# Banded attention with a routed expert layer: the key copy moves from VectorE to ScalarE, and two pieces of work change places

## The chip, the cores and the metric

The kernel runs on one core of a Trainium2 chip. The metric is device time in microseconds (us). Five engines work side by side, each through its own queue in program order: PE (TensorE, matrix products and transposes into the accumulator memory PSUM), DVE (VectorE), ACT (ScalarE), POOL (GpSimd, which also issues the gathers and scatters here) and SP (SyncE, which issues the loads). They wait for each other through semaphores. Buffers come from pools: a pool with three buffers lets the fourth tile start only when the first is no longer read.

## The reference

Two layers follow each other. The first is attention with a causal band of 96 keys, plus the first 8 keys for everyone, and a bias that falls with distance; the second sends each token to one of eight experts.

```python
# q, k, v: (4, 8, 768, 64): batch, heads, tokens, width
scores = (q @ k.T) / sqrt(64) + bias         # kept only where the key is global or local
a = exp(scores - max) / (sum + 1e-9)
x = (a @ v) as (3072, 512)                   # tokens by heads*width
logits = x @ w_gate                          # (3072, 8)
e = argmax(logits); gate = softmax(logits)[e]
out = gate * (relu(x @ w1[e]) @ w2[e])       # w1: (8, 512, 1024), w2: (8, 1024, 512)
```

## The kernel before

Tokens are taken in 24 blocks of 128 (N = 24), six to a batch (NBLK = 6). A block looks at its own keys (t = 1 in the tiles) and at the block before it (t = 0; a copy `ka` in which the first 32 columns hold the first keys of the batch). The first block of a batch has only t = 1. The loop is software-pipelined: step n makes scores of block n, prepares queries and keys of block n + 1, makes values of block n - 1 and tokens (rows of x, and logits) of block n - 2.

```python
def prep_q(n):                      # transpose on PE, copy out of PSUM on ACT
    transposed(ps_t, qts[n][:], rawt[n]["q"], "act", QS)

def prep_k(n):
    # ...
    transposed(ps_t, kts[n][:], rawt[n]["k"], "dve")      # L242 is the DVE copy in it
    # ...                           # for most blocks POOL then copies kts into ka (L294, L295)

def transposed(ps, dst, src, on, scale=1.0):
    pt = ps.tile([P, NPAIR, P], F32, tag="t", name="pt")  # one of 3 PSUM buffers "t"
    for m in range(NPAIR):
        nc.tensor.transpose(pt[:, m, :], src[...], ident[:])
    if on == "act":
        nc.scalar.activation(dst, pt[:], AF.Copy, bias=0.0, scale=scale)   # L240
    else:
        nc.vector.tensor_copy(out=dst, in_=pt[:])                          # L242

def scores(n):                      # two groups g of four heads
    # ... products into PSUM tile sp (L358), then on DVE:
    nc.vector.tensor_tensor(z, sc, bi, ALU.add)           # bias, p <- sp (L372), 128x1024
    ps[n].append(p)

def exps(n):
    for p in ps[n]:
        nc.scalar.activation(z, z, AF.Exp)                # L379, one for each group

def both(n):                        # the sums' addends: t = 0 and t = 1 added, on DVE
    if n % NBLK == 0:
        return
    for p in ps[n]:
        nc.vector.tensor_tensor(t, z[:, :, 0, :], z[:, :, 1, :], ALU.add)  # pb (L388)

def values(n):
    for m in range(NPAIR):
        # ... products p x v into po, a PSUM buffer "t", two m to a buffer (L400)
        if m % 2:
            nc.scalar.copy(ots[n][:, m - 1:m + 1], po[:, 0:2])             # L404
    pr = ps_r.tile(...)             # the only PSUM buffer "r"
    # ... sums of the exponentials from pb into pr (L410), logits from ots into pr (L414)
    nc.scalar.copy(rs[:], pr[:, 0, :])                    # L417

def tokens(n, rs):
    nc.tensor.transpose(pr[:, 1, :], rs[:], ident[:])     # L425
    # ... four transposes of ots into px (L428), a PSUM buffer "t"
    # ... on DVE: den, rden, lh (L434, L436, L439: den and lh read pr), lg (L442), xr <- px (L445)
```

The step before the change, cut to what matters. `choose` and `gates` pick the expert of a finished batch, `dispatch` ranks its tokens, and `send` scatters two blocks of rows to their experts' places in memory.

```python
for n in range(N + 1):
    if n < N: scores(n)
    if n + 1 < N: prep_q(n + 1)
    if n < N and n != 1: exps(n)
    if n == 2: both(1)
    if n == 0: biases(1, (0, 1, 2, 3), "act")
    # ... n == 2: memory is cleared on POOL; n == 3: ex.numbers, nine small DVE operations
    if n + 1 < N: prep_k(n + 1)
    # ... load(n + 3), pieces of the experts' weights, send()
    if n >= 2: tokens(n - 2, rs.pop(n - 2))      # and gates() at a batch's turn
    if n < N and n != 1: both(n)
    if n == N:
        ex.x_in_s(0, ps_t.tile(...))             # the early tile: transposes (L791), copy to xsT
    if n: rs[n - 1] = values(n - 1)
    if n == 1: exps(n)
    if n < N: mix_v(n)                           # POOL puts the first rows of v into a block
    # ... n == 22: send(); ex.early(), which gathers the early tile's rows into xs
    # ... dispatch at a batch's turn
# ... tokens(N - 1), and then the experts, beginning with
ex.up_s(0, 0, ex.xsT[0], ex.u[0])                # L800: the early tile's first products
```

The "early tile" holds up to 128 rows of expert 0, and a second one those of expert 1, from the first three batches, so that PE can begin on them while the last batch is still being dispatched.

Of the kernel before, what the change touches and what calls it, by code (L numbers as in the profile page):

```python
# [23 lines left out]
def kernel(  # L24
# [208 lines left out]
    def transposed(ps, dst, src, on, scale=1.0):  # L233

        pt = ps.tile([P, NPAIR, P], F32, tag="t", name="pt")
        for m in range(NPAIR):
            nc.tensor.transpose(pt[:, m, :], src[:, 2 * m:2 * m + 2, :].rearrange("p a d -> p (a d)"),  # L237
                                ident[:])
# [4 lines that stand above are left out]
# [7 lines left out]
    def banded(stack, rt, pool, rows, ex, den_all):  # L250
# [6 lines left out]
        ps_t = stack.enter_context(tc.tile_pool(name="ps_t", bufs=3, space=bass.MemoryType.PSUM))  # L257
        ps_r = stack.enter_context(tc.tile_pool(name="ps_r", bufs=1, space=bass.MemoryType.PSUM))

        rawt, kts, kas, qts, vts, ps, ots, prs, seqs = {}, {}, {}, {}, {}, {}, {}, {}, {}  # L260
        pbs = {}
        N = B * NBLK

        def load(n):
            b, i = divmod(n, NBLK)

            kind = dict(tag="vt0") if i == 0 else dict(tag="vt", bufs=6)
            vts[n] = seq.tile([P, H, D], F32, name="vt", **kind)
            r = rawt[n] = {}
            for nm, src in (("q", q), ("k", k)):  # L270
                r[nm] = raw.tile([P, H, D], F32, tag=nm, name=f"raw_{nm}")
                nc.sync.dma_start(out=r[nm][:], in_=src[b, :, ts(i, P), :].rearrange("h p d -> p h d"))
            nc.sync.dma_start(out=vts[n][:], in_=v[b, :, ts(i, P), :].rearrange("h p d -> p h d"))

        def mix_v(n):

            i = n % NBLK
            if i > 1:
                nc.gpsimd.tensor_copy(out=vts[n - 1][0:GW], in_=vts[n - i][0:GW])

        def prep_q(n):
            qts[n] = raw.tile([P, NPAIR, P], F32, tag="qt", bufs=2, name="qt")
            transposed(ps_t, qts[n][:], rawt[n]["q"], "act", QS)

        def prep_k(n):
            b, i = divmod(n, NBLK)
            kind = dict(tag="kt0") if i == 0 else dict(tag="kt", bufs=3)
            kts[n] = seq.tile([P, NPAIR, P], F32, name="kt", **kind)
            transposed(ps_t, kts[n][:], rawt[n]["k"], "dve")
            if i == 0:  # L290
                kas[n + 1] = kts[n][:]
            elif i + 1 < NBLK:
                t = raw.tile([P, NPAIR, P], F32, tag="ka", bufs=2, name="ka")
                nc.gpsimd.tensor_copy(out=t[:, :, GW:P], in_=kts[n][:, :, GW:P])  # L294
                nc.gpsimd.tensor_copy(out=t[:, :, 0:GW], in_=kts[n - i][:, :, 0:GW])  # L295
                kas[n + 1] = t[:]
# [36 lines left out]
        def biases(which, heads, on):  # L333
            for h in heads:
                g, j, a = h // 4, h // 2 % 2, h % 2
                dst, src = ((first[:, g, a, j], dist[:, 0]) if which == 0 else
                            (other[:, g, a, j], dist[:, 1:3]))
                if on == "act":
                    nc.scalar.activation(dst, src, AF.Copy, bias=0.0, scale=-slopes[h])
                else:  # L340
                    nc.gpsimd.tensor_scalar(dst, src, -slopes[h], None, ALU.mult)
# [30 lines left out]
                    nc.vector.tensor_tensor(z, sc, bi, ALU.add)  # L372
                ps[n].append(p)

        def exps(n):
            for p in ps[n]:
                z = p[:].rearrange("p a j t c -> p (a j) t c")
                z = z[:, :, 1, :] if n % NBLK == 0 else p[:].rearrange("p a j t c -> p (a j t c)")
                nc.scalar.activation(z, z, AF.Exp)  # L379

        def both(n):
# [4 lines that stand above are left out]
                t = work.tile([P, 2, 2, P], F32, tag="pb", bufs=4, name="pb")  # L386
                z = p[:].rearrange("p a j t c -> p (a j) t c")
                nc.vector.tensor_tensor(t[:].rearrange("p a j c -> p (a j) c"), z[:, :, 0, :], z[:, :, 1, :],  # L388
                                        ALU.add)
                pbs.setdefault(n, []).append(t[:])  # L390

        def values(n):
            vals = [(t, vts[n - 1 + t]) for t in range(n % NBLK == 0, 2)]
            ots[n] = work.tile([P, NPAIR, P], F32, tag="ot", name="ot")
            for m in range(NPAIR):
                if m % 2 == 0:
                    po = ps_t.tile([P, NPAIR, P], F32, tag="t", name="po")
                for x, (t, vt) in enumerate(vals):
                    for a in range(2):
                        nc.tensor.matmul(po[D * a:D * a + D, m % 2, :], lhsT=vt[:, 2 * m + a, :],  # L400
                                         rhs=ps[n][m // 2][:, a, m % 2, t, :], start=(x == 0),
                                         stop=(x == len(vals) - 1), skip_group_check=True)
                if m % 2:
                    nc.scalar.copy(ots[n][:, m - 1:m + 1], po[:, 0:2])  # L404

            pr = prs[n] = ps_r.tile([P, 4, P], F32, tag="r", name="pr")
            all_p = pbs.pop(n, None) or [p[:, :, :, 1, :] for p in ps[n]]
            for a in range(2):
                for m in range(NPAIR):
                    nc.tensor.matmul(pr[GW * m:GW * m + GW, 0, :], lhsT=one_in[:, a, :],  # L410
                                     rhs=all_p[m // 2][:, a, m % 2, :], start=(a == 0),
                                     stop=False, skip_group_check=True)
            for m in range(NPAIR):
                nc.tensor.matmul(pr[GW * m:GW * m + GW, 0, :], lhsT=gate_w[:, m, :], rhs=ots[n][:, m, :],  # L414
                                 start=False, stop=True, skip_group_check=True)
            rs = work.tile([P, P], F32, tag="rs", name="rs")
            nc.scalar.copy(rs[:], pr[:, 0, :])  # L417
            del ps[n]
            return rs
# [45 lines left out]
        def send():  # L465
            for _ in range(min(2, len(sends))):
                sends.pop(0)()

        rs = {}
        for n in range(N + 1):  # L470
            if n < N:
                scores(n)
            if n + 1 < N:
                prep_q(n + 1)
            if n < N and n != 1:
                exps(n)
            if n == 2:
                both(1)
            if n == 0:
                biases(1, (0, 1, 2, 3), "act")  # L480
            if n == 2:
                numbers = ex.clear_s()
            if n == 3:
                ex.numbers(*numbers)
            if n in (3, 4):
                biases(0, range(4 * n - 12, 4 * n - 8), "pool")
            if n + 1 < N:
                prep_k(n + 1)
            if n == 0:
                spare = ps_r.tile([P, 512], F32, tag="r", name="spare")  # L490
                for _ in range(4):
                    nc.tensor.matmul(spare[:], lhsT=idle[:, 0:P], rhs=idle[:], start=True, stop=True)
            if n + 3 < N:
                load(n + 3)
            for load_ in feed.pop(n, ()):
                load_()

            if n - 2 < N - NBLK + 2:
                send()
            b, i = divmod(n - 2, NBLK)  # L500
            if n >= 2:
                tokens(n - 2, rs.pop(n - 2))
                if i == 0 and b:
                    xr, _, oh, gates = seqs[b - 1]
                    gates()
            if n < N and n != 1:
                both(n)
            if n == N:
                ex.x_in_s(0, ps_t.tile([P, NPAIR, P], F32, tag="t", name="pt"))
            if n:  # L510
                rs[n - 1] = values(n - 1)
            if n == 1:
                exps(n)
            if n < N:
                mix_v(n)
            if i == 2 and b == B - 1:
                send()
                ex.early()
            if i == 0 and b > 0:
                sends += dispatch(pool, ps_t.tile([P, 512], F32, tag="t", name="pr"), rt, xr, oh)  # L520
                if b == B - 1:
                    send()
# [807 lines left out]
```

## Time and profile before

The median of three runs is 521.93 us (521.83 to 522.01); the profiled execution spans 522.3 us.

| engine | busy us | share of the span | instructions |
|---|---|---|---|
| PE | 504.2 | 97% | 5019 |
| PE weight loads | 423.7 | 81% | 5019 |
| DVE | 327.5 | 63% | 688 |
| ACT | 147.5 | 28% | 298 |
| POOL | 188.4 | 36% | 285 |

The busy time of an engine is the union of its instructions' spans. PE's instructions overlap, and a busy PE need not be at its peak. The shares are an average over the attention part (to about 161 us), a passage (to 171 us) and the experts (to the end). A list of groups gives, for each line, engine and tile, the summed busy time and the mean of one instruction: on the whole span the key copy L242 and query copy L240 take 682 and 598 ns each, the bias add L372 1218 ns, an addend's add L388 761 ns, an exponential over 1024 columns 1050 ns. DVE's instructions overlap a little at their edges, so two bias adds in a row take 2.36 us.

The chain of waits is followed back from the last instruction: at each step to what released it, or to the instruction before it on its engine. "Issue" in it is time in which nothing that the profile shows was waited for.

### The profile page before, as it was taken

Reading aid. Unit: us, or ns where it says so; the run is one execution under the profiler, and the core shown is the slowest. Engines: PE = TensorE matmul, PEld = TensorE weight load, DVE = VectorE, ACT = ScalarE, POOL = GpSimd, SP = SyncE. Lnnn points to the kernel's source line nnn. Section 1 sums busy time; section 2 is a strip of 40 time slices with the busy share of each in tenths; the row PEclk is TensorE's granted clock in tenths of the full one; section 3 lists DMA queues with packets and bytes.
Section 4 is the critical chain, followed back from the end, with each engine's and each line's share of the span. In section 5 each row is a group of like instructions: output and inputs, shape, how many; then the busy total and the mean of one; then the engine's idle time right before and its main releaser. Section 6 shows DMA issues by size and latency. Waiting matters only on the chain.

```text
span 522.3 us, 12395 instructions
## 1 busy us (share of the span) xinstructions
PE 504.2 (97%) x5019; PEld 423.7 (81%) x5019; DVE 327.5 (63%) x688; ACT 147.5 (28%) x298; POOL 188.4 (36%) x285
## 2 busy tenths in 40 slices
PE   7999999999997999999999999999999999999994
PEld 4888888888885778679899879969969878996984
DVE  5898978978985656817778258326707804832741
ACT  3555545544542101212212112112201211211120
POOL 5431161161253465306366055115307304511503
PEclk9999999999998999999999999999999999999998
DMA  9999798799922222037083452028156007400101
GB/s 185 214 221 213 164 217 226 165 217 227 303 98 71 97 79 82 8 140 278 21 312 125 163 187 94 2 95 333 31 204 216 26 1 261 175 2 23 43 4 50
DMA packets 96332, 72.75 MB, mean 139 GB/s; under 512 B 79324, under 2 KB 79326, under 8 KB 96228
## 3 DMA queue, kind: packets, MB, share of 16 engines
q1 hardware_dynamic: 87808, 52.44, 36.8%
q0 software_dynamic: 7872, 19.01, 10.7%
q8 instruction: 54, 0.88, 0.7%
q14 instruction: 50, 0.41, 0.3%
q10 hardware_dynamic: 548, 0.02, 0.1%
HBM read 61.46 MB, written 14.73 MB: 146 GB/s over the span
## 4 chain that ended last, share of the span: by engine, by line
PE 79%; DVE 10%; issue 7%; DMA 1%; POOL 1%; POOLq 0%; ACT 0%; DVEq 0%; ACTq 0%
PE u L972 18%; PE u L800 10%; PE d L1034 9%; PE d L1043 7%; PE u L810 7%; PE sp L358 5%; PE po L400 5%; DVE p L372 5%; PE d L810 3%; PE u L1141 2%; PE u L1116 2%; PE pt L237 2%; PE pr L410 2%; DVE kt L242 2%; PE t L952 2%
## 5 line engine op out<-in xcount | busy, mean ns | idle before, releaser
L1050 DVE TENSOR_TENSOR UV<-UV,d 128x512 f32<-128x512 f32 x8 | 5.5, 688 | 110.9 <-ACT yu L1144 81.3
L734 POOL DMA_INDIRECT out_dram<-ys,to_u x8 | 8.3, 1039 | 142.6 <-ACT yu L1144 87.6
L372 DVE TENSOR_TENSOR p<-sp,other 128x1024 f32<-128x1024 f32 x40 | 47.0, 1218 | 16.6 <-PE sp L358 15.1
L800 PEld LDWEIGHTS u<-xsT,w 128*128 128x128 f32 x448 | 50.9, 192 | 1.8 <-DVE c L942 0.8
L400 PE MATMUL po<-p,vt 128*64 128x128 f32 x704 | 48.6, 284 | 3.7 <-DVE kt L242 3.0
L800 PE MATMUL u<-xsT,w 128*128 128x128 f32 x448 | 51.7, 276 | 0.0
L400 PEld LDWEIGHTS po<-p,vt 128*64 128x64 f32 x704 | 39.1, 140 | 11.8 <-DVE kt L242 7.0
L972 PE MATMUL u<-cx,c 128*128 128x128 f32 x384 | 48.1, 275 | 0.0
L379 ACT ACTIVATE p<-p 128x1024 f32<-128x1024 f32 (+1 forms) x48 | 45.1, 979 | 4.3 <-DVE p L372 3.0
L972 PEld LDWEIGHTS u<-cx,c 128*128 128x128 f32 x384 | 45.5, 192 | 0.0
L358 PE MATMUL sp<-qt,kt 64*128 64x128 f32 x448 | 39.0, 277 | 1.0 <-DVE kt L242 0.9
L972 PE MATMUL u<-xT,w 128*128 128x128 f32 x256 | 39.4, 276 | 0.2 <-issue 0.2
L972 PEld LDWEIGHTS u<-xT,w 128*128 128x128 f32 x256 | 34.2, 192 | 1.3 <-DVE y L1064 0.4
L810 PE MATMUL u<-w,huT 128*128 128x512 f32 x80 | 35.1, 592 | 0.0
L358 PEld LDWEIGHTS sp<-qt,kt 64*128 64x128 f32 x448 | 31.6, 188 | 3.1 <-issue 1.2
L1034 PE MATMUL d<-c,ch 128*128 128x256 f32 x128 | 32.8, 379 | 0.0
L215 POOL DMA_INDIRECT xs_dram<-xr,slot_i x24 | 25.0, 1042 | 19.3 <-DVE cnt L862 10.8
L294 POOL COPY ka<-kt 128x384 f32<-128x384 f32 x16 | 8.1, 506 | 65.2 <-DVE den_all L434 62.8
L810 PEld LDWEIGHTS u<-w,huT 128*128 128x128 f32 x80 | 15.2, 190 | 17.0 <-issue 16.7
L388 DVE TENSOR_TENSOR pb<-p 128x512 f32<-128x512 f32 x40 | 28.8, 761 | 0.0
L240 ACT ACTIVATE qt<-pt 128x512 f32<-128x512 f32 x24 | 14.4, 598 | 47.2 <-PE pt L237 44.7
L358 PE MATMUL sp<-qt,ka 64*128 64x128 f32 x256 | 27.4, 285 | 0.1
(254 smaller groups left out, 1026.2 us busy)
## 6 DMA issues: line engine op xcount, KB each, us to landing
w<-in_moe_w_dram SPq DMA_DIRECT2D x24, 1024.0 KB
w<-in_moe_w_dram SPq DMA_DIRECT2D x16, 512.0 KB
raw_q<-in_q_dram SPq DMA_DIRECT2D x24, 256.0 KB
raw_k<-in_k_dram SPq DMA_DIRECT2D x24, 256.0 KB
vt<-in_v_dram SPq DMA_DIRECT2D x24, 256.0 KB
xs_dram<-xr,slot_i POOLq DMA_INDIRECT x24
xg<-xs_dram,grow POOLq DMA_INDIRECT x16
mu<-xs_dram,grow_e POOLq DMA_INDIRECT x16
```

Source lines behind the costliest of these rows:

```text
L215: d = nc.gpsimd.indirect_dma_start(out=xs_dram[:], out_offset=bass.IndirectOffsetOnAxis(ap=slot_i[:, u:u + 1], axis=0), in_=xr[:, u, :].bi ...
L240: nc.scalar.activation(dst, pt[:], AF.Copy, bias=0.0, scale=scale)
L358: nc.tensor.matmul(sp[:, a, j, t, :], lhsT=kt[r, m, :], rhs=qts[n][r, m, :], start=True, stop=True, skip_group_check=True)
L372: nc.vector.tensor_tensor(z, sc, bi, ALU.add)
L379: nc.scalar.activation(z, z, AF.Exp)
L388: nc.vector.tensor_tensor(t[:].rearrange("p a j c -> p (a j) c"), z[:, :, 0, :], z[:, :, 1, :], ALU.add)
L400: nc.tensor.matmul(po[D * a:D * a + D, m % 2, :], lhsT=vt[:, 2 * m + a, :], rhs=ps[n][m // 2][:, a, m % 2, t, :], start=(x == 0), stop=(x ...
L800: nc.tensor.matmul(ph[:, i, :], lhsT=self.w[e % 2][0][:, c, ts(half * HF + i, P)], rhs=xT[:, c, :], start=(c == 0), stop=(c == NDC - 1), s ...
L810: nc.tensor.matmul(py[:].rearrange("p a b -> p (a b)"), lhsT=h[:, f, :], rhs=self.w[e % 2][1][:, f, :], start=(f == 0), stop=(f == NFC - 1 ...
L972: nc.tensor.matmul(bank[:, r, :], lhsT=lhs(k), rhs=rhs(k), start=first, stop=True, skip_group_check=True)
L1034: nc.tensor.matmul(self.half(i, j), lhsT=lhs, rhs=rhs, start=(f == 0 and j == 0), stop=True, skip_group_check=True)
L1043: nc.tensor.matmul(self.half(i, j), lhsT=lhs(f), rhs=rhs(f), start=False, stop=True, skip_group_check=True)
```

## The change

Three things move. The copy of the transposed keys out of PSUM goes from DVE to ACT for all blocks but the first, to relieve DVE, whose copy stood behind the bias adds. The sums' addends (`both`) are made one step later, ahead of the token chain, when their exponentials are long done; the second group's exponential goes behind the copies of the values and the sums on ACT. And at the end the early tile's transposes go behind the last block's values, so that PE works on those values while the gather is under way.

```diff
-            transposed(ps_t, kts[n][:], rawt[n]["k"], "dve")
+            transposed(ps_t, kts[n][:], rawt[n]["k"], "act" if n else "dve")
 ...
-        def exps(n):
-            for p in ps[n]:
+        def exps(n, groups):
+            for p in ps[n][groups]:
 ...
-            if n < N and n != 1:
-                exps(n)
-            if n == 2:
-                both(1)
-            if n == 0:
-                biases(1, (0, 1, 2, 3), "act")
             if n == 2:
                 numbers = ex.clear_s()
             if n == 3:
                 ex.numbers(*numbers)
             if n in (3, 4):
                 biases(0, range(4 * n - 12, 4 * n - 8), "pool")
+            if 0 < n <= N:
+                both(n - 1)
             if n + 1 < N:
                 prep_k(n + 1)
+            if n < N and n != 1:
+                exps(n, slice(0, 1 if n else 2))
+            if n == 0:
+                biases(1, (0, 1, 2, 3), "act")
 ...
-            if n < N and n != 1:
-                both(n)
+            if n:
+                rs[n - 1] = values(n - 1)
+            if 0 < n < N:
+                exps(n, slice(n != 1, 2))
             if n == N:
                 ex.x_in_s(0, ps_t.tile([P, NPAIR, P], F32, tag="t", name="pt"))
-            if n:
-                rs[n - 1] = values(n - 1)
-            if n == 1:
-                exps(n)
```

In the changed kernel ACT's order in a step is: query copy, key copy, first exponential, two output copies, sums' copy, second exponential. DVE's is: two bias adds, two addends' adds of the block before, the token chain.

## The prediction

> **What bounds the kernel now.** I read the busy shares first, then stretches of the span, then the chain of waits, then the list of waits. The page's first part gives PE 97% of the span, with DVE at 63% and ACT at 28%, so the first question is where the missing 3% of PE lie. The stretches tell (columns: stretch, its length, then busy us of PE, PEld, DVE, ACT, POOL with counts of instructions, the granted PE clock, the DMA share and GB/s):
>
> ```profile
> 33.00:40.00 7.00, 7.00 (x109) 6.28 (x107) 6.59 (x11) 4.05 (x8) 1.09 (x1) 1.00 0.90 221
> ...
> 101.00:108.00 7.00, 6.50 (x103) 5.60 (x103) 6.79 (x18) 3.38 (x6) 1.73 (x3) 1.00 0.61 120
> ...
> 161.00:167.00 6.00, 3.46 (x29) 2.82 (x29) 2.90 (x10) 0.27 (x1) 3.46 (x4) 0.81 0.33 88
> 167.00:171.00 4.00, 3.58 (x52) 3.14 (x49) 0.68 (x4) 1.01 (x3) 0.00 (x0) 0.87 0.00 0
> 171.00:522.00 351.00, 343.38 (x2681) 288.99 (x2679) 187.98 (x371) 65.08 (x145) 130.21 (x170) 1.00 0.32 113
> ```
>
> The reader is to see three regimes. Attention up to 161 us has PE full, but in some stretches DVE is as full (6.79 of 7 at 101 to 108). At 161 to 171 PE stands still for some 3 us and then runs at a clock of 0.81 to 0.87. From 171 on the experts keep PE at 98%; nothing of the change lies there, so whatever is gained before 171 moves the end by as much.
>
> The chain of waits shows what ends last in the first two regimes (columns: start, us, what):
>
> ```profile
> 103.09 0.92 DVE p L372
> 104.01 0.14 issue
> 104.14 1.21 DVE p L372
> 105.35 0.61 DVE kt L242
> 105.97 0.04 issue
> 106.01 1.09 PE po L400 x16
> 107.10 0.57 PE pr L410 x16
> ...
> 160.76 3.50 DMA xs<-xs_dram,grow_s
> 164.27 0.14 issue
> 164.40 0.85 PE pt L791 x4
> 165.26 3.29 PE po L400 x32
> 168.55 0.57 PE pr L410 x16
> ```
>
> In step 15 (scores of block 15) the chain leaves PE: two bias adds on DVE, then the key copy behind them in DVE's queue, and only then the second half of the values' products, whose PSUM buffer the key copy had to free. Near the end the gather of the early tile's rows lands at 164.27, its transposes follow, and the last block's values stand behind them though their inputs were ready long before. The list of waits up to 170 us (who waited for whom: us in total, times, longest) names the same two:
>
> ```profile
> PE po L400 <- DVE kt L242: 3.0, 7, 0.8
> PE pt L791 <- DMA xs<-xs_dram,grow_s: 2.1, 1, 2.1
> ```
>
> **What the skill says.** The Trainium skill, "SBUF — State Buffer", section "Who interferes with whom", has it that a DVE instruction with two SBUF inputs contends with a GpSimd instruction that reads SBUF. The addends' add (L388) is such a one, and the trace agrees: a pair takes 1.28 us alone (107.34) but 1.59 us at 81.85, beside POOL's copy of the values at 81.69. "ScalarE: Activation LUTs", section "Table sets: the hidden batching unit", says that copy is in every table set, so a copy between two exponentials costs no switch; the trace agrees, as queries are copied by ACT (0.60) and exponentials follow without a gap. "TensorE: Matmul & The Clock Gate", section "Part 1: The HAM clock gate", says that an idle PE falls to half its clock; here 3 us of waiting brought the mean clock to 0.81, and 32 products of the values took 3.29 us where 1.90 is usual.
>
> **The change part by part.** PE's work in a full step, from the chain at 30 to 43 us, where PE alone is on it: scores 1.99, transposes of q and k 1.02, of sums and outputs 0.11 and 0.44, values 1.90, sums 0.57, logits 0.31: 6.34 us, and full steps there follow each other at 6.33 (30.22, 36.55). Later full steps take 6.85 to 7.05 (100.86, 107.92, 114.92, 121.96), a full set of six 39.5 (54.49 to 94.03).
>
> First, the key copy leaves DVE. DVE's step is two bias adds 2.36, key copy 0.61, the token chain (0.09, 0.21, 0.24, 0.27, 0.60, with gaps 1.55) and two addends' adds 1.20: 5.7 us, 5.1 without the copy. The two steps at each batch's turn add 1.1 (choice of expert) and 1.8 (gates and ranks). ACT's step grows from 3.6 (query copy 0.55, exponentials 1.95, three copies 1.0) to 4.2 of 6.3, so it doesn't bind.
>
> Second, the addends. They now stand between the bias adds and the token chain, 1.20 us earlier than that chain, and in place of 0.61. So the last read of the sums' bank by the token chain (lh, L439) ends some 0.6 later in a step than now: before 4.73 after the step's start, after 5.33. PE wants that single bank for the next sums at 5.45. It just fits; any DVE delay over 0.1 us lands on PE there. This is my main doubt: the wait for the key copy can come back as a wait for the bank.
>
> Third, the second exponential goes behind the copies of values and sums in ACT's queue, so these no longer stand behind two exponentials. In the first step after a batch's turn (the short values, 6.16 us where PE has 5.4) the outputs' copy starts 5.13 into the step only because of this; after: query and key copies to 3.9, one exponential to 4.9, copy. Gain 0.25 in three steps.
>
> Sum over attention. Start: block 1's scores waited 0.6 to 0.9 for the key copy behind the first bias adds: 0.6 gained. Step 2 took 7.33 with the copy late: gains 0.65, as 0.35 of the 1.0 returns through POOL's copies of the same key, which start at about 4.0 now and meet the addends. Step 3 has nine small DVE operations (0.85) ahead of the addends now: loses 0.4. Together 0.85. In each later set of six: 0 in the half step, 0.25 in the next, 0 and 0.1 in the two with POOL's key copies beside the addends, 0.5 and 0 in the two with scatters, where the bias add starts only 2.1 into the step instead of 1.2. There bank arithmetic gives 2.1 + 2.36 + 1.20 + 0.65 = 6.3, past 5.45, so about today's 7.0 stays in one of them. That is 0.85 for a set, and with two sets and a part (0.4) before step 22: 0.85 + 1.7 + 0.4 = about 2.9.
>
> Fourth, the tail. Now the values of the last block (3.29), sums and logits (0.9) and the wait for their copy stand between the transposes at 164.40 and the experts' first product at 170.46. After, they come before the transposes. From the start of step 22 (147.47) I count 6.6 and 7.2 for steps 22 and 23 with the bank's wait, then 0.5 for the copy of the sums, 0.55 transposes, 1.9 values, 0.95 sums and logits: transposes at 165.2. The gather follows the values of block 21, whose products end 0.8 earlier in their step, so it lands at about 163.5 and is hidden. Then 0.44 for transposes at full clock and 0.7 for DVE's copy, under which the last token's transposes lie: experts from about 166.3, against 170.5. Gain 4.2, besides the 2.9. The experts' chain of dispatch follows the same products as before, so it moves along.
>
> Total 4.2 + 2.9 = 7.1; 521.9 - 7.1 = 514.8, taken as 514.7.
>
> **Rivals.** (a) The bank binds in all the full steps: PE waits for the sums' bank where it waited for the key copy, attention gains nothing, only the tail is left: 517.7. For it: only 0.1 us of slack, and a collision costs 0.3. Against it: without scatters or POOL copies DVE has over a microsecond free in a step. (b) DVE's relief comes through: all steps run at PE's 6.34, with 6.6 at the turn. That is about 39.5 - 37.5 = 2 a set, some 5.5 in attention, and the last steps too are nearer PE's own work, so that the tail gives 5: 511.5. For it: stretches such as 33 to 40 with PE at 7.00 of 7. Against it: the late bias adds beside scatters have another cause than the key copy. (c) Loads bind once steps shrink: 1.28 MB in a step with a piece of weights takes 6 us at the 213 to 221 GB/s of the early slices. But loads are issued three steps ahead and only one wait on keys is listed, so under 1 us. (d) PE goes on waiting for the gather because scatters do not come earlier: transposes can't precede 163.5, costing nothing unless attention gains over 2 more.
>
> **Range and chances.** Tail alone gives 517.7; a tail spoilt by 1 us, 518.7; all at PE's pace 511.5, a little better with the wait at 164 gone 510.8. I put 8 in 10 on 510.8 to 518.7. Faster by over 2% needs 511.5 or less, the whole of rival (b): 0.17. Within 2%: 0.80. Slower by over 2% would need 10 us lost, which no row suggests: 0.03.
>
> **What would show it.** Right: the key copy no longer ends waits of the values' products; the first expert product starts near 163.5 (166.3 less 2.9); the clock stays at 1.00 through the tail; the wait for the gather is near nothing. The bank: waits of the sums (L410) for lh or pb, some 0.3 to 0.8 each in steps with scatters or key copies on POOL. Wrong: steps of 6.4 beside scatters (then faster), sums waiting in every step (then 517 or more), or experts that don't follow the earlier start because a gather or a weight load takes over after 171.

## The result and the profile after

The changed kernel takes 515.35 us (median of five runs, 514.19 to 516.26) against 522.01 us (521.83 to 522.22) for the kernel before: ratio 0.9873, 95% interval 0.9856 to 0.9891. Predicted were 514.7 us, in a range of 510.8 to 518.7.

One caution comes first. The profiled executions are single ones: that of before spans 522.3 us and took 524.06 us in all, 2.05 above the median; that of after spans 514.3 us and took 516.22, 0.87 above its median. So the two traces stand 8.0 us apart and the medians 6.7. The extra 1.3 us belong to the executions, and the differences below, which come from the traces, are by so much too large in sum.

The busy shares (first part of the page, kernel after):

```profile
PE 498.3 (97%) x5019; PEld 423.2 (82%) x5019; DVE 313.2 (61%) x665; ACT 159.4 (31%) x321; POOL 189.4 (37%) x285
```

Twenty-three copies moved from DVE to ACT: DVE has 14.3 us less work and ACT 11.9 more. PE's share is 97% as before, and its instructions are as many, yet they count 5.9 us less busy time; only 2.1 of the 8.0 us are idle time that went. PE's instructions overlap, so when they follow each other more slowly they can still leave no gap, and the busy share hides the wait: step 7 took 6.16 us before and 5.70 after, with no more than 0.03 us idle in either. The counts in the stretches show it. Step 16, one with scatters, before:

```profile
108.00:115.00 7.00, 6.96 (x103) 5.94 (x103) 5.52 (x11) 3.39 (x6) 4.42 (x6) 1.00 0.76 189
```

The same step after, and what follows it (columns as in the prediction):

```profile
104.00:111.00 7.00, 7.00 (x124) 6.14 (x115) 5.28 (x10) 4.08 (x8) 4.58 (x7) 1.00 0.92 215
...
155.00:160.00 5.00, 3.62 (x33) 3.38 (x35) 2.11 (x7) 1.28 (x2) 2.99 (x3) 0.66 0.40 105
160.00:165.00 5.00, 4.82 (x61) 4.13 (x58) 2.76 (x13) 0.88 (x3) 0.00 (x0) 1.00 0.01 3
165.00:514.00 349.00, 341.65 (x2666) 287.40 (x2665) 186.47 (x365) 65.07 (x144) 129.21 (x170) 1.00 0.33 114
```

PE counts as busy for all but 0.04 of the 7 us in both, but in them it now gets through 124 instructions in place of 103. (The stretch 101 to 108 in the prediction is step 15, one with POOL's key copies.) The end of attention keeps a hole: 3.62 of 5 us at 155 to 160, at a clock of 0.66. From 165 on nothing has changed: from the experts' first product to the end are 351.8 us before and 351.6 after.

The list of waits up to 175 us (after) names what PE waits for now:

```profile
PE pr L410 <- DVE lh L439: 4.3, 9, 1.1
...
PE po L400 <- POOL vt L279: 1.4, 1, 1.4
```

The waits of the values for the key copy (3.0 us) and of the transposes for the gather (2.1 us) are gone. In their place stand nine waits of the sums for the last read of their only bank (in steps 2, 3, 8, 9, 14, 15, 20, 21 and 23), and one wait for a copy on POOL. The second is seen in the chain at the end of attention (after; start, us, what):

```profile
153.24 0.35 POOL xs L724
...
154.60 1.33 POOL xs L724
155.94 1.16 POOL vt L279
...
157.15 3.31 PE po L400 x32
160.46 0.57 PE pr L410 x16
161.03 0.31 PE pr L414 x6
161.34 0.60 PE pt L789 x4
161.97 0.70 DVE xsT L790
...
162.71 3.84 PE u L798 x32
```

The two gathers of the early tiles are issued at 153.24 and 154.60. The copy that puts the first rows of v into the last block stands behind both in POOL's queue and ends at 157.10; only then do the last values start. The trace of before already has this copy behind both gathers (POOL, before):

```profile
160.76 1.17 POOL L726 DMA_INDIRECT xs<-xs_dram,grow_s  x1 [3.72 <-DVE xr L445]
162.24 1.00 POOL L726 DMA_INDIRECT xs<-xs_dram,grow_s  x1 [0.30 <-issue]
163.25 0.62 POOL L279 COPY vt<-vt 32x512 f32<-32x512 f32 x1
```

It ended at 163.87 there, 0.4 us before the gather landed.

Laid out by steps (from one step's first scores to the next one's; computed from the start times in the two traces), the gain before step 22 is 5.6 us, 0.2 of it ahead of step 2:

| step | before us | after us | what lies in it |
|---|---|---|---|
| 2 and 3 | 7.33, 6.96 | 6.58, 7.38 | first key copies; nine small DVE operations in step 3 |
| 4, 5 | 6.34, 6.34 | 6.34, 6.34 | nothing besides |
| 7, 13, 19 | 6.16 each | 5.70 each | short values |
| 8, 14, 20 | 6.85, 6.84, 6.85 | 6.84 each | key copies on POOL, choice of expert |
| 9, 15, 21 | 7.00, 7.05, 7.06 | 6.64, 6.77, 6.83 | key copies on POOL |
| 10, 11, 16, 17 | 7.04, 7.04, 7.00, 7.03 | 6.34, 6.33, 6.34, 6.34 | scatters |

From the start of step 22 to the experts' first product are 23.0 us before (147.47 to 170.46) and 20.8 after (141.89 to 162.71): 2.2 us more.

### The profile page after: what moved, and what is told of

Its sections match the earlier page's. It is cut to its first block, busy times and chain, and to the rows that moved or that the text cites. A ratio compares the mean times of both kernels' runs of the same rounds, so it can differ in the third digit from the quotient of the medians.

```text
span 514.3 us, 12403 instructions
## 1 busy us (share of the span) xinstructions
PE 498.3 (97%) x5019; PEld 423.2 (82%) x5019; DVE 313.2 (61%) x665; ACT 159.4 (31%) x321; POOL 189.4 (37%) x285
## 4 chain that ended last, share of the span: by engine, by line
PE 82%; DVE 10%; issue 6%; POOL 1%; POOLq 0%; DVEq 0%
PE u L970 18%; PE u L798 10%; PE d L1032 9%; PE d L1041 7%; PE u L808 7%; PE sp L358 6%; PE po L400 5%; DVE p L372 4%; PE pt L237 3%; DVE pb L388 3%; PE d L808 3%; PE u L1139 3%; PE u L1114 3%; PE pr L410 2%; PE t L950 2%
## 5 line engine op out<-in xcount | busy, mean ns | idle before, releaser
L379 ACT ACTIVATE p<-p 128x1024 f32<-128x1024 f32 (+1 forms) x48 | 47.3, 988 | 1.4 <-DVE p L372 1.1
L400 PE MATMUL po<-p,vt 128*64 128x128 f32 x704 | 45.1, 281 | 1.4 <-POOL vt L279 1.4
L358 PE MATMUL sp<-qt,kt 64*128 64x128 f32 x448 | 37.9, 275 | 0.9 <-DVE kt L242 0.9
L215 POOL DMA_INDIRECT xs_dram<-xr,slot_i x24 | 23.8, 993 | 17.9 <-DVE cnt L860 9.9
L294 POOL COPY ka<-kt 128x384 f32<-128x384 f32 x16 | 9.2, 576 | 56.2 <-ACT kt L240 56.2
L997 ACT COPY uv<-u 128x256 f32<-128x256 f32 x32 | 11.9, 373 | 51.2 <-PE u L970 51.1
L1032 PEld LDWEIGHTS d<-c,ch 128*128 128x128 f32 x128 | 24.3, 190 | 3.3
```

The lines of the kernel that those rows point to most:

```text
L215: d = nc.gpsimd.indirect_dma_start(out=xs_dram[:], out_offset=bass.IndirectOffsetOnAxis(ap=slot_i[:, u:u + 1], axis=0), in_=xr[:, u, :].bi ...
L358: nc.tensor.matmul(sp[:, a, j, t, :], lhsT=kt[r, m, :], rhs=qts[n][r, m, :], start=True, stop=True, skip_group_check=True)
L1032: nc.tensor.matmul(self.half(i, j), lhsT=lhs, rhs=rhs, start=(f == 0 and j == 0), stop=True, skip_group_check=True)
```

## The experiments

Twelve runs follow, four on each of three chips; each is compared with runs of the kernel before on the same chip (medians 522.93, 523.67 and 521.80 us). Of these chips the changed kernel itself ran on the third alone. Three questions: do the parts of the change need each other, what is the reorder of the early tile worth, and why do the steps with scatters run at PE's pace?

**The key copy alone.** The kernel before with only this edit:

```diff
-            transposed(ps_t, kts[n][:], rawt[n]["k"], "dve")
+            transposed(ps_t, kts[n][:], rawt[n]["k"], "act" if n else "dve")
```

> The kernel before with one line of the change: keys copied by ACT, all else as before. Theory (the parts of the change need each other): in ACT's queue the key copy now stands behind both exponentials and ends some 5.8 us into the step, so the second half of the values' products, which takes the key's PSUM buffer, starts there instead of at 4.5, and full steps take about 7.5 us: 530 to 540 us in all. Rival (the relief of DVE carries the attention's gain by itself): steps near 6.4, 515 to 518 us.

Measured: 540.36 us, ratio 1.0322 (1.0274 to 1.0369), at the upper end of what was expected: the copy alone costs 17 us. The waits up to 165 us (key copy alone) show where:

```profile
PE po L400 <- DVE xr L445: 13.1, 15, 1.8
PE po L400 <- ACT kt L240: 3.0, 5, 1.1
```

In the chain of this kernel one exponential runs at 67.58 and the key copy at 68.53, some 5.1 us into its step, because both exponentials stand before it in ACT's queue. The transposed keys hold one of the three PSUM buffers until that copy ends. In 15 of these 20 waits the second half of the values' products starts as soon as `xr` has read the tokens' buffer, so it seems to take that one instead: in step 5 this read ends at 5.04 us, where the key copy ended at 4.16 in the kernel before. The split of the exponentials is no extra; without it the copy must not move.

**The other moves without the copy.** The changed kernel with the key copy back on DVE:

```diff
-            transposed(ps_t, kts[n][:], rawt[n]["k"], "act" if n else "dve")
+            transposed(ps_t, kts[n][:], rawt[n]["k"], "dve")
```

> The changed kernel with the key copy given back to DVE. Theory: DVE does bias adds, addends, key copy and then the token chain; the key copy ends 5.4 into the step and the last read of the sums' bank 6.0, so full steps take about 7.2 us: 524 to 530 us. Rival (it was only the addends and their meeting with the scatters that cost time): 515 to 517 us.

Measured: 530.72 us, ratio 1.0136 (1.0093 to 1.0179), a little more than expected. The chain (changed kernel with keys on DVE) shows a full step:

```profile
68.12 1.05 PE po L400 x16
...
69.25 0.38 ACT ot L404
69.63 0.04 issue
69.67 1.09 PE po L400 x16
```

Now the key copy stands behind the two addends on DVE, its buffer is still held, and PE must wait for the copy of its own first outputs before it can go on (0.5 us in the step shown; 8.6 us in 15 times up to 165 us). So the copy and the new order of the loop each lose alone, and win only together.

**The early tile's reorder alone.** The kernel before with the transposes of the early tile moved behind the last values:

```diff
-            if n == N:
-                ex.x_in_s(0, ps_t.tile([P, NPAIR, P], F32, tag="t", name="pt"))
             if n:
                 rs[n - 1] = values(n - 1)
             ...
+            if n == N:
+                ex.x_in_s(0, ps_t.tile([P, NPAIR, P], F32, tag="t", name="pt"))
```

> The kernel before with the early tile's transposes behind the last block's values, nothing else. Theory (POOL's copy of the first value rows stands in its queue behind the two gathers, so the last values cannot start before it): gain of 0.5 to 1.5 us, 520.5 to 521.5 us, with PE waiting for vt instead of for the gather. Rival (the tail is worth what was predicted, 4.2): 517 to 518 us.

Measured: 521.97 us against 522.93, ratio 0.9975 (0.9957 to 0.9993): 1 us. The chain (reorder alone) gives the reason in two lines:

```profile
163.54 0.63 POOL vt L279
...
164.21 3.57 PE po L400 x32
```

The values no longer wait for the gather's data, but for POOL to get past the gathers' issue to the copy behind them, which is hardly earlier: 164.21 where the transposes began at 164.40 before.

**The change without that reorder.** The changed kernel with the transposes ahead of the values again ran on two chips.

```diff
+            if n == N:
+                ex.x_in_s(0, ps_t.tile([P, NPAIR, P], F32, tag="t", name="pt"))
             if n:
                 rs[n - 1] = values(n - 1)
             ...
-            if n == N:
-                ex.x_in_s(0, ps_t.tile([P, NPAIR, P], F32, tag="t", name="pt"))
```

> The changed kernel with the early tile's transposes put back ahead of the last block's values. Theory (same): within 0.7 us of the changed kernel, 515 to 516.5 us. Rival (the move brings 2 to 4 us): 517.5 to 519.5 us.

On the first chip: 520.96 us, ratio 0.9962 (0.9946 to 0.9978), outside both expectations: a much smaller gain than the change's, and by more than the reorder could explain. Its trace showed why: the steps with scatters (10, 11, 16, 17, 22) took 6.84, 7.49, 7.87, 7.65 and 6.83 us. So the run does not measure the reorder, and it raised the third question. On the third chip it ran again, beside the changed kernel itself:

> The changed kernel itself, beside its variants on one chip. Theory (the stall beside the scatters depends on the run or the chip, not on the order of the variant): here the steps of blocks 10, 11, 16, 17 and 22 also take more than 6.34 us, by 0.5 to 1.5 each, and the time is 517 to 521 us, above the 515.35 of its first runs. Rival (the stall came from the edits of the variants, as none of their runs was free of it): steps of 6.34 and 515 to 516 us.

> The changed kernel with the early tile's transposes ahead of the last block's values again, beside the changed kernel on the same chip. The passage alone was worth 1 us on the kernel before (521.97 against 522.93). Theory: here it is worth 0 to 2 us: 0 to 2 us slower than the changed kernel, because values that wait for POOL's copy or for a late step give part of it back. The prediction's own figure was 4.2 slower.

The changed kernel: 515.33 us (514.05 to 517.38), ratio 0.9881 (0.9861 to 0.9901), as in its first runs and not the 517 to 521 of the theory. Without the reorder: 516.28 us (515.25 to 519.22), ratio 0.9907 (0.9884 to 0.9929). The same program took 520.96 on the first chip, so its edit is not what stalls the steps with scatters. The intervals overlap; the medians lie 0.95 us apart, and the traces 0.6 us at the start of the experts' first product (161.95 and 161.32). Without the reorder (chain, third chip) the transposes wait for the gather's data:

```profile
153.24 3.40 DMA xs<-xs_dram,grow_s
156.63 0.14 issue
156.77 0.63 PE pt L789 x4
157.40 1.05 PE po L400 x16
...
162.11 3.57 PE u L798 x32
```

With it (the changed kernel, same chip) the values wait for POOL's copy and start 0.3 us before that:

```profile
155.89 1.16 POOL vt L279
...
157.10 1.97 PE po L400 x32
...
161.32 3.84 PE u L798 x32
```

So the reorder is worth about 1 us: in the kernel before that is clear of the noise, in the changed kernel it is not. Most of the 4.2 is not in it.

**The copy between the gathers.** The changed kernel with the second gather issued behind the last values' copy on POOL:

```diff
-            for e in range(NS):
-                self.gather(self.xs[:, e, :], self.grow_s[:, e:e + 1])
+            self.gather(self.xs[:, 0, :], self.grow_s[:, 0:1])
...
+            if n == N - 1:                       # behind mix_v(n) and early()
+                ex.gather(ex.xs[:, 1, :], ex.grow_s[:, 1:2])
```

> The changed kernel with POOL's copy of the first value rows for the last block put between the two gathers of the early tiles; the second gather, needed much later, is issued after it. Theory (that copy's place in POOL's queue holds the last values up, 1.4 us of wait and then products at a low clock, 3.3 us for 1.9): last values start near 155.6, early tile's first product near 160, gain of 2 to 3.5 us over the changed kernel: 512 to 513.5 us. Rival (the last values are held by the second exponential or the sums' copy, or PE would be cold anyway): within 0.7 us of 515.3.

Measured on the second chip: 522.76 us, ratio 0.9972 (0.9957 to 0.9988): a clear miss. Its steps with scatters took 6.90, 7.62, 8.70, 7.75 and 6.86 us, so PE came to the last values only at 164.09, long after POOL's copy, and the edit had nothing to gain. It is judged in the last kernel below.

**The addends before POOL's key copies.** The changed kernel, with POOL reading a corner of the second addend before it copies keys, so that the two no longer overlap:

```diff
+                if n - 2 in pbs:
+                    nc.gpsimd.tensor_copy(out=scr[:], in_=pbs[n - 2][1][:, 0, 0, 0:8])
                 nc.gpsimd.tensor_copy(out=t[:, :, GW:P], in_=kts[n][:, :, GW:P])
```

> The changed kernel in which POOL first reads a corner of the addends (eight columns, a tiny copy) before it copies the keys for the next block, so that its copies no longer run beside the addends' adds. Theory (two readers of SBUF, DVE's two-input add and POOL, shut each other out for 0.3 us, and the token chain then frees the sums' bank late): in steps 2, 8, 14 and 20 and the steps after the turn, the pair of adds takes 1.28 instead of 1.59 us, the sums start near 5.5 instead of 5.8 to 6.0, 1.5 to 2.5 us less: 513 to 514 us. Rival (the bank's wait is not set by that meeting, or the later key copy delays the next scores): 515 to 517 us.

Measured on the second chip: 520.74 us, ratio 0.9942 (0.9925 to 0.9960), well above both expectations. In the aimed steps the theory held: steps 2, 8 and 9 went from 6.58, 6.84 and 6.64 to 6.34, 6.60 and 6.34 us, and a pair of addends from 1.59 to 1.28 us. This is what the Trainium skill, "SBUF — State Buffer", section "Who interferes with whom", leads one to expect, and 0.3 us a pair is its size here. But the steps with scatters took 7.62, 7.17, 10.25, 7.43 and 7.64 us, and ate it.

**Where the scatters lie.** Two kernels, each run once on the second chip, ask whether it matters when in a step a scatter is issued. In the kernel before, POOL was made to wait for the next queries, so that the scatters of the first two batches come in the middle of a step:

```diff
-            if n - 2 < N - NBLK + 2:
+            if n - 2 < N - NBLK + 2 and (n % NBLK != 3 or n > 18):
+                if sends and n < 18:
+                    nc.gpsimd.tensor_copy(out=scr[:], in_=qts[n + 1][:, 0, 0:8])
                 send()
```

> The kernel before in which the scatters of batches 1 and 2 are moved inside the step: not in steps 9 and 15 but in 10, 11, 12 and 16, 17, 18, and in 10, 11, 12, 16 and 17 POOL first reads a corner of the query copy, so that they run at about 3.4 to 6 us of the step, away from the addends' adds at 6.5 to 7.8. The third batch's scatters stay where they were. Theory (a scatter that meets an addends' add holds up what other engines learn of PE by 1 to 2 us): in steps 10, 11, 16 and 17 the first bias add starts 1.2 into the step and these steps take 6.3 to 6.5 instead of 7.0, while steps 22 and 23 keep 2.1: 519 to 520 us. Rival (scatters delay PE's signals wherever they lie): bias adds still late or other waits in the same steps, 521 to 523 us.

Measured: 529.05 us, above both expectations. The late bias adds of steps 10, 11, 16 and 17 went (1.21 us into the step in place of 2.1), but the steps grew to 7.18, 7.87, 7.80 and 7.86 us. Steps 22 and 23, whose scatters had not moved, kept 2.1. What is late now is ACT's second copy of the values' outputs: it starts 6.41, 7.10, 7.03 and 7.09 us into these steps, though PE's products end at 5.52, as in step 5, where the copy starts at 5.57. In the changed kernel POOL was made to wait for the next keys, which puts the scatters beside the addends:

```diff
+                if sends and n % NBLK in (4, 5):
+                    nc.gpsimd.tensor_copy(out=scr[:], in_=kts[n + 1][:, 0, 0:8])
                 send()
```

> The changed kernel in which, in steps 10, 11, 16, 17 (and 22), POOL first reads a corner of the key copy, so that the scatters start at about 4.0 into the step, beside the addends' adds at 3.5 to 4.8. Theory (meeting of scatter and addends' add): the adds take 1.5 or more, a scatter 1.2 instead of 0.98, signals of PE reach ACT or DVE 1 us late, and these four steps take 6.7 to 7.4 instead of 6.34: 516.5 to 519 us. Rival (only a port is shared for 0.3 us): the steps take at most 6.6, 515 to 516.5 us.

Measured: 518.66 us, steps 10, 11, 16, 17 and 22 at 7.51, 6.83, 6.86, 6.86 and 6.84. These are the times expected from a meeting of scatters and addends, but not its signs: in steps 10 and 16, where the two meet, a pair of adds takes 1.29 and 1.28 us, as it does alone. And the bias adds are late (1.8) in steps 10, 16 and 22, which still have a scatter 0.1 to 0.35 us after their start, and on time (1.21) in steps 11 and 17, whose scatters all come at 4.7 and later. There it is again ACT's second copy that is late. Step 11 (begins at 74.40; timeline of PE, POOL and ACT):

```profile
77.96 1.97 PE L401 MATMUL po<-p,vt 128*64 128x128 f32 x32
...
79.09 0.98 POOL L215 DMA_INDIRECT xs_dram<-xr,slot_i  x1 [0.48 <-issue]
...
80.46 0.37 ACT L405 COPY ot<-po 128x256 f32<-128x256 f32 x1 [0.94 <-PE po L401]
```

and the same step of the changed kernel (begins at 73.31; after):

```profile
76.86 1.97 PE L400 MATMUL po<-p,vt 128*64 128x128 f32 x32
...
78.87 0.37 ACT L404 COPY ot<-po 128x256 f32<-128x256 f32 x1 [0.45 <-PE po L400]
```

PE's products end 5.52 us into the step in both; the copy follows at 6.06 in the one and 5.57 in the other. So in these two kernels, each run once, the delay goes where the scatters go, and a meeting with the addends is not needed for it.

The same for the bias add is seen when one step of the same loop is compared on two chips. Step 17, without the reorder of the early tile, first chip (timeline: start, us, engine, line, operation; in brackets how long the engine stood idle, and for whom):

```profile
113.93 0.49 PE L358 MATMUL sp<-qt,ka 64*128 64x128 f32 x4
...
114.92 0.39 PE L358 MATMUL sp<-qt,ka 64*128 64x128 f32 x4
114.94 0.97 POOL L215 DMA_INDIRECT xs_dram<-xr,slot_i  x1 [0.30 <-issue]
...
116.51 2.36 DVE L372 TENSOR_TENSOR p<-sp,other 128x1024 f32<-128x1024 f32 x2 [2.62 <-PE sp L358]
```

and the changed kernel, third chip:

```profile
110.68 0.49 PE L358 MATMUL sp<-qt,ka 64*128 64x128 f32 x4
...
111.89 2.36 DVE L372 TENSOR_TENSOR p<-sp,other 128x1024 f32<-128x1024 f32 x2 [1.31 <-PE sp L358]
112.00 0.97 POOL L215 DMA_INDIRECT xs_dram<-xr,slot_i  x1 [0.30 <-issue]
```

PE makes the scores in the same time in both; the bias add follows 2.6 us after their start on the first chip and 1.2 us on the third. DVE was idle and waited for PE's signal alone. Steps 4 and 5, which have no scatters beside them, are at 6.34 us in both traces.

**The scatters two steps later.** The changed kernel with the scatters of the first two batches sent beside blocks 12, 13, 18 and 19:

```diff
-            if n - 2 < N - NBLK + 2:
+            if n - 2 < N - NBLK + 2 and n not in (9, 10, 15, 16):
                 send()
```

> The changed kernel with the scatters of the first two batches sent two steps later, so that their traffic lies beside blocks 12, 13, 18 and 19, whose steps have spare time on DVE. Theory (PE's signals come late while the scatters' traffic runs, wherever it lies): steps 10, 11, 16 and 17 go to 6.34 us even if they stall in the changed kernel on this chip, and steps 12, 13, 18 and 19 grow by 0 to 1 us each; in sum 0 to 3 us faster than the changed kernel. Rival (the late bias adds of those steps have another cause than the scatters, say the loads that lie there): steps 10, 11, 16, 17 stay as they are in the changed kernel.

Measured: 518.15 us (515.22 to 519.53), ratio 0.9915 (0.9887 to 0.9943), so 2.8 slower than the changed kernel on this chip, where 0 to 3 faster was expected. The question itself got no answer, since on this chip the changed kernel's steps 10, 11, 16, 17 and 22 were at 6.34 us with the scatters in them. Most of the loss is a new wait (chain, scatters later):

```profile
129.27 7.12 DMA xs_dram<-xr,slot_i
...
136.70 0.69 DVE xr L445
```

The rows of the next but one batch go into the buffer that the late scatter still reads; DVE waits 1.9 us for it in step 21, which takes 8.68 us in place of 6.84, and 0.7 us at the end of step 14, after which step 15 takes 7.21 in place of 6.77.

**All together.** The last kernel has the later scatters, the key copies behind the addends, the small operations of step 3 behind the values, and the last values' copy between the gathers; the edits are those above, and

```diff
-            if n == 3:
-                ex.numbers(*numbers)
...
             if n:
                 rs[n - 1] = values(n - 1)
+            if n == 3:
+                ex.numbers(*numbers)
```

> The kernel of the shifted scatters, and beside that POOL's key copies made to wait for the addends, the nine small operations of step 3 moved behind the values, and the last values' copy on POOL placed between the two early gathers. Theory: the bank's waits vanish, 0.24 to 0.5 us in each of eight steps, 1.0 in step 3, and up to 1.2 at the tail where the steps before it come without delay: 3 to 5 us faster than the kernel with only the scatters shifted. Rival (another wait takes their place): within 1.5 us of it.

Measured: 512.79 us (512.00 to 513.95), ratio to before 0.9833 (0.9817 to 0.9850). That is 5.4 us faster than the kernel with the later scatters alone (3 to 5 were expected), and 2.5 faster than the changed kernel on the same chip, with no run of the one in the range of the other. Of the bank's nine waits two are left (list of waits up to 175 us):

```profile
PE pr L413 <- DVE lh L442: 2.3, 2, 1.5
```

and POOL's copy is out of the way (timeline of POOL):

```profile
152.11 1.05 POOL L729 DMA_INDIRECT xs<-xs_dram,grow_s  x1 [2.77 <-DVE den_all L437]
153.17 0.61 POOL L280 COPY vt<-vt 32x512 f32<-32x512 f32 x1
153.95 1.30 POOL L729 DMA_INDIRECT xs<-xs_dram,grow_s  x1 [0.17 <-issue]
```

The copy ends at 153.78, 6.7 us after the start of step 23, where it was 8.9 in the changed kernel (157.05 less 148.17). By steps against the changed kernel on this chip: step 2 gains 0.25, step 3 1.04, steps 8, 9, 14, 15 and 20 0.24 to 0.37 each (1.39 in sum), the tail after step 23's start 1.46 (13.15 to 11.69), the start 0.14; step 21 loses 1.73. Sum 2.5, which is what the medians say. The loss in step 21 (8.57 us) is that of the later scatters. A kernel without that edit wasn't run; with step 21 at the 6.40 us of the kernel with late key copies it would be estimated at 512.79 - 2.17 = 510.6 us.

## Why the prediction came out right

The total was right because two of its terms were off in opposite directions: attention gave 2.7 us more than predicted, the tail 2.0 less. That these nearly cancelled was luck.

- **Key copy off DVE: right.** The waits of the values for it are gone, and the copy costs ACT 23 x 0.59 us, which bind nothing. (The parts of ACT's step add up to 3.5, not 3.6; nothing hangs on it.) What the prediction did not say is how much this hangs on the split exponentials: the copy alone lost 17 us.
- **The addends and the bank: right, in place and size.** The last read of the bank ends 5.34 us into an undisturbed step (predicted 5.33), PE there at 5.48 without waiting; with POOL's copy beside the addends the read ends at 5.64 and PE waits 0.3. Step 3 loses 0.42 (predicted 0.4). The kernel with late key copies removed the seven of these waits that lie in steps with such copies.
- **Short values: too small.** 0.46 in each of three steps, not 0.25. Key-copy steps gained 0.23 to 0.36 in one of each two, not 0.1; block 1's start gave 0.2, not 0.6, against this trace of before. (In the traces of the two experiments that keep its loop up to there, step 2 begins 0.6 and 1.2 us later than in it, so this term is uncertain.)
- **Scatter steps: the term of attention that was mis-sized.** The prediction kept "about today's 7.0" in one of two, because the bias add would start 2.1 us in, for a cause of its own. It started at 1.21, all ran at 6.34, and four steps gave 2.76 us in place of 1.0: the prediction's own sign of being wrong, "steps of 6.4 beside scatters". Rival (b) had it here, and its 5.5 us for attention too. The objection against it, that the late bias adds have another cause than the key copy, holds: in the kernel before they went when the scatters moved, and on two other chips variants of the changed loop had late bias adds in these very steps. Why the changed kernel was free of them, in its first runs and on the third chip, and its variants on the other two were not, is open; this term depends on the chip, or on something that went with it.
- **Attention in all:** 5.6 us in the traces against 2.9. Up to 1.3 of it may be owed to before's profiled execution being a long one.
- **The tail: the step that failed.** The prediction read that the last block's values stand behind the transposes "though their inputs were ready long before", and took nothing else to be in their way. In the trace of before one of these inputs, POOL's copy of the first rows of v, was ready only 0.4 us before the gather landed, since the gathers are also instructions in POOL's queue. So the reorder by itself is worth only about 1. From the start of step 22 the prediction counts 14.85 us to the last values, 1.9 for their 32 products and 2.1 for the rest, a gain of 4.2. Both traces of the changed kernel have the last values at 15.26: PE came 1.4 us earlier, as steps 22 and 23 were shorter than counted, and waited for that copy. The products then took 3.31 us in the trace shown above, 1.97 in that of the third chip. With that the tail gained 2.2 and 3.5 against the same trace of before; in the first, 1.4 of the 2.0 that are missing are these slow products, and 0.4 the later start. Moving the copy forward, among the edits of the last kernel, brought the last values to 13.87 and let the tail gain 1.46 more.
- **"The clock stays at 1.00 through the tail": wrong in one trace, right in another.** PE was busy 3.62 of 5 us from 155 to 160 in both traces of the changed kernel, after the same 1.4 us of waiting, but at a clock of 0.66 in the one shown above and 1.00 in that of the third chip: 32 products took 3.31 and 1.97 us. The Trainium skill, "TensorE: Matmul & The Clock Gate", section "Part 1: The HAM clock gate", calls the clock's warm-up run-variable because the window that watches PE's activity runs freely; these two traces of one program fit that.
- **After 171 us:** all moved along, to 0.2 us.

## What to carry to other kernels

A copy moved to another engine takes that engine's place in the queue with it: ask what stands before it there and which buffer it holds meanwhile, and move these first. When a gather's data is no longer waited for, look at its issue: small copies behind it in the issuing engine's queue are the next wait. And a step with 0.1 us of slack is a place where a collision of 0.3 us between two engines costs nearly all of that (0.24 to 0.3 us in steps 2, 8 and 9 here), so it can be worth making the engine that isn't on the path wait.

A busy share near 100% doesn't rule out waits either: count the instructions in a stretch.

## What was unexpected

In steps beside scatters PE's signals can reach DVE and ACT late: 1.4 us late in step 17 on the first chip, while PE's own products run at their usual pace. In step 16 of the kernel with late key copies, which took 10.25 us, the second bias add started only 2.6 us after the last product of its scores had ended. The trace of before shows the same: in step 10 the first four heads' scores end at 1.16 us, as in step 5, and DVE is free from 0.71 on, but the bias add starts at 2.12. The changed kernel without the early tile's reorder took 519.92 to 522.59 us on one chip and 515.25 to 519.22 on another, with its five scatter steps at 36.7 us in all on the first and 31.7 on the second. Not so the kernel before, whose medians on all chips lie within 2 us. Why the signals are late, and why the changed loop is free of it on some chips and not on others, was not settled; no kernel without scatters was run.
